# A two-layer MLP by Strassen products on one core: the second pair's first layer made two-level, its block sums made earlier by VectorE and GpSimd, rectifications moved to ScalarE

## The chip, the core and the metric

The kernel runs on one core of a Trainium2 chip. A core has TensorE (PE; the profile lists its weight loads apart, as PEld), VectorE (DVE), ScalarE (ACT), GpSimd (POOL) and SyncE (SP), whose queue issues most of the DMAs here. Each engine works through its own instructions in order and waits on semaphores for the others. The metric is device time in microseconds; lower is better. Three runs of the kernel before took 793.56, 793.8 and 795.42 us, median 793.8.

## What is computed

The reference is a block of linear attention followed by a Fourier mixing layer with an MLP. Cut to what matters here:

```python
x = lightning_attn(q, k, v, lam)            # (4, 8, 768, 64) -> (4, 768, 512)
u = x + real(fft(fft(x, axis=1), axis=2))
un = (u - mean(u)) / sqrt(var(u) + 1e-06)   # over the last axis
out = u + np.maximum(un @ w_ch1, 0.0) @ w_ch2   # w_ch1 512 x 2048, w_ch2 2048 x 512
```

All of it is float32. The change concerns the last line alone, for the last two thirds of the rows.

## The kernel before

**Stages.** Attention, Fourier mixing and normalisation give 12 groups of 256 rows each (`ORDER`). Four of them (`PLAIN`) go through the MLP by ordinary matmuls while the mixing of the others still runs (`mlp`). The other eight (`LATE`) are kept in DRAM, normalised (`utd`) and not (`ud`), and are worked at the end as four pairs, j = 0 to 3, of 512 rows. From here on the chip does nothing but the MLP of these pairs.

**One level.** A pair is one matrix product per layer, and each matrix is cut in 2 x 2 blocks. `PRODUCTS` names the seven block products of Strassen's scheme (in Winograd's form), each of a block or block sum of one matrix with one of the other. `combine_weights` makes the weights' block sums once: `s2.A` holds the first layer's blocks (w1: a11, a12, a22, s1 to s4), `s2.B` the second's.

**Two levels.** A product can itself be done by seven smaller ones. That needs sums of quarters of every one of the seven operands (S1, S2, S4 of the left, T1, T2, T4 of the right; the fourth, S3 or T3, replaces a quarter). `DEEP = 2` tells which pairs do the first layer in one level: j < DEEP does (`first_layer`), j >= DEEP uses two levels (`deep_first`). The second layer always has two levels (`deep_second`). `seven` is the frame of a two-level product: seven steps m = 0 to 6 in three PSUM banks X, Y, Z. X takes m = 0, 2, 4, 6 one on top of the other, and after each step the bank is read out by ScalarE (a copy, where the destination is fresh) or VectorE (an addition).

**first_layer(j).** Its loop runs over HF = 8 slices i of the hidden units. A slice has seven products of two matmuls each (128x128 by 128x256; the profile records two passes of each, so 28 records a slice). In PE's order a slice runs: a11, a12 (of slice i), s4, a22*t4 (of slice i-1, in `finish`), s2, s3, s1 (of slice i). Bank X collects a11, s2, s1, s4, and ScalarE copies X out after each of the first three; Z collects s3 and a22*t4; Y takes a12. VectorE adds Y to a11 (L915), Z to a22 (L924) and later Z to a12 (L903), rectifies each in place (L916, L925, L904: `tensor_scalar` with max), and makes s1 = a21 + a22 and s3 = a11 - a21 (L905, L906) from a21, which ScalarE rectified out of X into an SBUF tile `sv` (L901). In slices 5 to 7 VectorE also does `split` (L856, 128x512: a quarter difference in place), and at the end `prepare_a(j, 0)` and `prepare_a(j, 1)` (L870, L872, L874), the quarter sums that the first two second-layer products need.

**The weights' quarter sums.** They serve every pair and are made once, by GpSimd, beside the first layers: `keep_sums` (L727, L731) for the second layer's seven operands in pair 0's first layer, `keep_sums_w` (L747) for the first layer's seven in pair 1's. Each is four 128x512 operations for a product, seven products, so 28. Three results of four (all four in `keep_sums_w`) go through six rotating buffers `tx` to DRAM (`td`, `sd`) by SP's queue, and come back by `load_three` just before use. S3 goes back into a quarter of the weights (`place_sums_w`). GpSimd starts after `begun`, a copy of one column that waits for pair 0's first a11.

**Order.** `in_step` interleaves consecutive products: while product q does its steps 4 to 6, product q+1 does its first. So PE's order at the start of a second layer is, with qP,m for product P and step m: q0,0; q0,1; q0,2; q0,3; q1,0; q0,4; q1,1; q0,5; q1,2; q0,6; q1,3; q2,0; q1,4; and so on, eight records each. `late` puts pair 0's first and second layer, pair 1's first and second layer, and the deep pairs 2 and 3 behind each other. Tile pools with one buffer (`y2`, the pair's output tile that `open_y` takes; `ur`, its input) make the next user of a buffer wait until the last one is through.

Of the kernel before, what the change touches and what calls it, by code (L numbers as in the profile page):

```python
# [76 lines left out]
def kernel(  # L77
# [642 lines left out]
    s2.td = []  # L720
    s2.begun = wt.tile([128, 1], F32, name="begun")

    def keep_sums(k):

        pin = tc.keep_in_program_order
        B11, B12, B21, B22 = quarters_b(s2.B[PRODUCTS[k][1]])
        pin(nc.gpsimd.tensor_tensor(B12, B22, B12, op=SUB))  # L727
        T1, T2, T4 = t = [new(s2.yp, [128, HF // 2, HM // 2], "tx", bufs=6) for _ in range(3)]
        s2.td.append([dram.tile([128, HF // 2, HM // 2], F32, name=f"td{k}{i}") for i in range(3)])
        for i, o, x, y, op in ((1, T2, B12, B11, ADD), (0, T1, B22, T2, SUB), (2, T4, B21, T2, SUB)):  # L730
            pin(nc.gpsimd.tensor_tensor(o, x, y, op=op))  # L731
            nc.sync.dma_start(s2.td[k][i], o)

    s2.sd = []

    def quarters_w(t):

        return [t[:, k, f:f + FH // 2] for f in (0, FH // 2) for k in range(2)]

    def keep_sums_w(k):  # L740

        pin = tc.keep_in_program_order
        A11, A12, A21, A22 = quarters_w(s2.A[PRODUCTS[k][0]])
        S3, S2, S1, S4 = [new(s2.yp, [128, FH // 2], "tx", bufs=6) for _ in range(4)]
        s2.sd.append([dram.tile([128, FH // 2], F32, name=f"sd{k}{i}") for i in range(4)])
        for i, o, x, y, op in ((3, S3, A11, A21, SUB), (1, S2, A22, S3, SUB), (0, S1, S2, A11, ADD), (2, S4, A12, S2, SUB)):
            pin(nc.gpsimd.tensor_tensor(o, x, y, op=op))  # L747
            nc.sync.dma_start(s2.sd[k][i], o)

    def place_sums_w():  # L750

        for k, (a, _) in enumerate(PRODUCTS):
            nc.sync.dma_start(quarters_w(s2.A[a])[2], s2.sd[k][3])
# [22 lines left out]
    DEEP = 2  # L776
# [107 lines left out]
    def first_layer(j):  # L884
# [11 lines left out]

        def finish(i, X, Z):
            a11, a12, a22, s1, s3 = (h[n][:, :, i, :] for n in ("a11", "a12", "a22", "s1", "s3"))
            prod(X, "s4", "b22", i, False)
            a21 = new(s2.hp, [128, G, 128], "sv", bufs=3)  # L900
            nc.scalar.activation(a21, two(X), AF.Relu)  # L901
            prod(Z, "a22", "t4", i, False)
            V.tensor_tensor(a12, two(Z), a12, op=ADD)  # L903
            V.tensor_scalar(a12, a12, 0.0, None, op0=ALU.max)  # L904
# [3 lines left out]
        last = None  # L908
        for i in range(HF):
            a11, a12, a22 = (h[n][:, :, i, :] for n in ("a11", "a12", "a22"))  # L910
            X, Y, Z = (bank()[:, 0:G * 128] for _ in range(3))
# [4 lines left out]
            V.tensor_scalar(a11, a11, 0.0, None, op0=ALU.max)  # L916
            if last:
                finish(*last)
            prod(X, "s2", "t2", i, False)
            nc.scalar.copy(a12, two(X))  # L920
            prod(Z, "s3", "t3", i, True)
            prod(X, "s1", "t1", i, False)
            nc.scalar.copy(a22, two(X))
            V.tensor_tensor(a22, two(Z), a22, op=ADD)  # L924
            V.tensor_scalar(a22, a22, 0.0, None, op0=ALU.max)  # L925
            last = (i, X, Z)
            if j < min(DEEP, 2) and i < len(PRODUCTS):
                if i == 0:
                    tc.keep_in_program_order(nc.gpsimd.tensor_copy(s2.begun, h["a11"][:, 0, 0, 0:1]))
                (keep_sums, keep_sums_w)[j](i)  # L930
# [7 lines left out]
        run(prepare_a(j, 0))  # L938
        finish(*last)
        run(prepare_a(j, 1))  # L940
# [22 lines left out]
    def deep_first(j, k):  # L963
# [37 lines left out]

        if k == 1:
# [145 lines left out]
    def late():  # L1148
        for j in range(PAIRS):
            if j < DEEP:  # L1150
                open_pair(j)
                if j == 0:
                    run(inputs(0))
                first_layer(j)
                if j + 1 < DEEP:
                    in_step(second_layer(j) + [(inputs(j + 1), iter(()))])
# [116 lines left out]
```

## Time and profile before

The profiled execution took 796.12 us; its span, from the first to the last instruction, is 793.9 us, and the granted TensorE clock was 0.995 on average.

| engine | busy us | share of the span | instructions |
|---|---|---|---|
| PE | 763.4 | 96% | 5616 |
| DVE | 585.5 | 74% | 1148 |
| ACT | 225.4 | 28% | 532 |
| POOL | 197.6 | 25% | 198 |

| stretch, us of the span | length | PE busy | DVE busy | ACT busy | POOL busy |
|---|---|---|---|---|---|
| pair 0 first layer, 425.34 to 476.31 | 50.97 | 50.67 | 48.26 | 12.27 | 39.03 |
| pair 0 second layer, 476.31 to 518.29 | 41.98 | 41.98 | 30.98 | 3.99 | 6.56 |
| pair 1 first layer, 518.29 to 568.49 | 50.20 | 50.20 | 43.66 | 12.28 | 38.76 |
| pair 1 second layer, 568.49 to 607.79 | 39.30 | 39.30 | 31.30 | 3.99 | 7.08 |

The granted clock is 1.00 in all four stretches. A row of the timeline gives start, duration, engine, line, operation, output and input, shape and count, and in brackets the idle time of the engine before it with what ended that. [...]

### The profile page before, as it was taken

To read this page: it belongs to the slowest core of one execution; us is meant where nothing else is said; L and a number is where in the kernel's file an instruction comes from. 1 tells how busy PE (TensorE), PEld (TensorE's weight loads), DVE (VectorE), ACT (ScalarE), POOL (GpSimd) and SP (SyncE) were. 2 spreads that over 40 slices of the span, in tenths; PEclk is the share of its full clock that TensorE was granted. 3 is DMA by queue.
4 is the path that set the end of the run, shared out by engine and by line. 5 is a ranking of instruction groups with operands and counts; after the bars stand their busy time and mean duration, and the time that the engine had idled before them with its cause. 6 is when DMAs were issued, how large, how long until landed. Compare 5 with 4: busy or idle time off the path is not lost.

```text
span 793.9 us, 14617 instructions
## 1 busy us (share of the span) xinstructions
PE 763.4 (96%) x5616; PEld 646.3 (81%) x5616; DVE 585.5 (74%) x1148; ACT 225.4 (28%) x532; POOL 197.6 (25%) x198
## 2 busy tenths in 40 slices
PE   6889989999999999998999999999999999999995
PEld 5768766758585867767946889988999999999995
DVE  6899889675844582345698998769966699758983
ACT  3665443335621221321201221022211342034300
POOL 3223330011111110211004950279205001220021
PEclk9999999999999999999999999999999999999998
DMA  9978723238842147441233374345944455455341
GB/s 243 247 165 245 196 85 129 85 74 205 227 116 77 54 79 146 108 143 64 54 66 107 133 246 162 97 167 191 348 147 153 150 174 185 129 176 186 121 131 70
DMA packets 152331, 116.80 MB, mean 147 GB/s; under 512 B 113998, under 2 KB 113998, under 8 KB 152262
## 3 DMA queue, kind: packets, MB, share of 16 engines
q1 hardware_dynamic: 147120, 103.39, 45.8%
q0 software_dynamic: 2112, 6.69, 2.4%
q10 hardware_dynamic: 3030, 5.78, 2.0%
q8 instruction: 45, 0.74, 0.4%
q14 instruction: 24, 0.20, 0.1%
HBM read 83.58 MB, written 32.25 MB: 146 GB/s over the span
## 4 chain that ended last, share of the span: by engine, by line
PE 78%; DVE 9%; DMA 4%; issue 4%; ACT 1%; POOL 1%; SPq 0%; POOLq 0%; ACTq 0%; DVEq 0%
PE p L1046 21%; PE p L891 12%; PE p L976 11%; PE pm L658 10%; PE pm L644 9%; PE pa L525 3%; PE pa L300 3%; PE pa L341 3%; DMA x<-xb,ix 2%; PE pa L335 2%; PE pa L276 1%; PE pa L357 1%; PE pa L320 1%; DVE sc L304 1%; PE pa L281 1%
## 5 line engine op out<-in xcount | busy, mean ns | idle before, releaser
L644 PE MATMUL pm<-ut,w 128*128 128x256 f32 x512 | 119.7, 384 | 0.0
L658 PE MATMUL pm<-w,hr 128*128 128x512 f32 x256 | 115.7, 596 | 0.2 <-DVE w L227 0.2
L644 PEld LDWEIGHTS pm<-ut,w 128*128 128x128 f32 x512 | 95.6, 192 | 14.2 <-issue 2.1
L658 PEld LDWEIGHTS pm<-w,hr 128*128 128x128 f32 x256 | 46.6, 190 | 49.3 <-issue 48.0
L1060 POOL TENSOR_TENSOR y<-y,u 128x512 f32<-128x512 f32 x12 | 18.8, 1569 | 199.2 <-DVE y L1069 156.8
L1046 PE MATMUL p<-tx,sx 128*128 128x128 f32 x416 | 54.9, 275 | 0.0
L1046 PEld LDWEIGHTS p<-tx,sx 128*128 128x128 f32 x416 | 50.6, 192 | 0.0
L891 PE MATMUL p<-ur,w 128*128 128x256 f32 x192 | 46.9, 379 | 0.1
L272 POOL TENSOR_TENSOR kd<-k,decay 128x512 f32<-128x512 f32 x20 | 22.0, 1100 | 95.3 <-PE pa L320 48.7
L1052 ACT COPY y<-p 128x128 f32<-128x128 f32 x48 | 12.8, 266 | 104.1 <-PE p L1046 103.8
L1054 DVE TENSOR_TENSOR y<-p,y 128x128 f32<-128x128 f32 x92 | 25.5, 286 | 22.5 <-PE p L1046 15.9
L891 PEld LDWEIGHTS p<-ur,w 128*128 128x128 f32 x192 | 36.3, 190 | 5.7 <-issue 0.5
L304 DVE TENSOR_TENSOR sc<-pa,decay 128x512 f32<-128x512 f32 x48 | 31.5, 683 | 8.1 <-PE pa L300 7.9
L1046 PE MATMUL p<-w,ha 128*128 128x128 f32 x288 | 37.4, 275 | 0.0
L300 PEld LDWEIGHTS pa<-qT,kT 64*128 64x128 f32 x384 | 26.1, 193 | 13.4 <-ACT qT L283 7.4
L652 ACT ACTIVATE hr<-pm 128x256 f32<-128x256 f32 x44 | 16.7, 385 | 66.2 <-PE pm L644 66.0
L1046 PEld LDWEIGHTS p<-w,ha 128*128 128x128 f32 x288 | 35.0, 192 | 0.2
L300 PE MATMUL pa<-qT,kT 64*128 64x128 f32 x384 | 30.8, 292 | 3.3 <-ACT qT L283 3.1
L341 PE MATMUL pa<-sc,v 128*64 128x128 f32 x384 | 30.0, 279 | 4.0 <-DVE sc L304 3.8
L558 POOL TENSOR_SCALAR ve<-mv 128x2 f32<-128x2 f32 x12 | 3.4, 286 | 122.3 <-DVE mv L555 122.3
L891 PE MATMUL p<-sx,w1s 128*128 128x256 f32 x128 | 32.9, 380 | 0.2 <-DVE sx L794 0.2
L650 DVE TENSOR_SCALAR hr<-pm 128x256 f32<-128x256 f32 x20 | 8.3, 414 | 32.8 <-PE pm L644 32.8
(234 smaller groups left out, 1736.6 us busy)
## 6 DMA issues: line engine op xcount, KB each, us to landing
tx<-td SPq DMA_DIRECT2D x84, 256.0 KB, 2.7
raw<-in_moe_w_ch_dram SPq DMA_DIRECT2D x32, 512.0 KB, 4.0
tx<-sd SPq DMA_DIRECT2D x42, 256.0 KB, 2.7
sd<-tx SPq DMA_DIRECT2D x28, 256.0 KB, 2.1
k<-in_k_dram SPq DMA_DIRECT2D x24, 256.0 KB, 5.2
q<-in_q_dram SPq DMA_DIRECT2D x24, 256.0 KB, 4.3
v<-in_v_dram SPq DMA_DIRECT2D x24, 256.0 KB, 5.0
td<-tx SPq DMA_DIRECT2D x21, 256.0 KB, 2.0
```

The source lines that it names most:

```text
L272: nc.gpsimd.tensor_tensor(kd, kt, kpow, op=ALU.mult)
L300: mm(pss[hi][:, hp, :], lhsT=kT[HD[hi], hp, :], rhs=qT[HD[hi], hp, :], start=True, stop=True)
L304: nc.vector.tensor_tensor(t, pss[hi], decay[:, hi::2, :], op=ALU.mult)
L341: mm(po[HD[hi], hp, :], lhsT=vt[:, 2 * hp + hi, :], rhs=sc[hi][:, hp, :], start=(c == 0 and hp == 0), stop=(hp == HP - 1), skip_group_chec ...
L525: mm = nc.tensor.matmul(ps[:, n, :], lhsT=piece(a, i, n), rhs=cs[0:rows, a, i in (2, 3), n, :], start=(a == 0), stop=(a == 1))
L644: nc.tensor.matmul(ps, lhsT=w1[:, c, 128 * fc:128 * fc + 128], rhs=ut[:, c, :], start=(c == 0), stop=(c == KO - 1))
L658: nc.tensor.matmul(ps, lhsT=hr[(fc - f0) // 4][:, fc % 4, 128 * i:128 * i + 128], rhs=w2[:, fc, :], start=(fc == f0), stop=(fc == f1 - 1))
L891: nc.tensor.matmul(ps, lhsT=s2.A[a][:, kt, 128 * i:128 * i + 128], rhs=U[b][:, kt, :], start=(first and kt == 0), stop=(kt == 1), skip_gro ...
L976: nc.tensor.matmul(ps[:, 128 * i:128 * i + 128], lhsT=ab[m][0][:, 128 * i:128 * i + 128], rhs=ab[m][1], start=(start and i == 0), stop=Tru ...
L1046: nc.tensor.matmul(ps[:, 0:HM // 2], lhsT=ab[m][0][i], rhs=ab[m][1][:, i, :], start=(start and i == 0), stop=(i == HF // 2 - 1), skip_grou ...
L1054: V.tensor_tensor(o, ps[:, 0:HM // 2], o, op=ADD)
L1060: nc.gpsimd.tensor_tensor(o, y, u, op=ADD)
```

## The change

- `DEEP` becomes 1: pair 1 is a deep pair like 2 and 3, and `first_layer` runs for pair 0 alone.
- The first layer's quarter sums (`sd`) have to exist one pair earlier. `block_sums` replaces `keep_sums` and `keep_sums_w`. In pair 0's first layer GpSimd still makes the second layer's 28, and then those of the first layer's products 3 and 4 (8 more). VectorE makes those of products 0, 1 and 5 (12 operations, two in each of slices 1 to 6). Those of products 2 and 6 are made by GpSimd when pair 1's first two deep products start (8 operations).
- The first-layer sums don't use `tx`. They are staged in a `y2` tile (`spare_y`), four slots that every product reuses, and go to DRAM from there on SP's queue.
- In `first_layer` the three rectifications of a slice move from VectorE to ScalarE (`relu`, 128x256 in SBUF). a21 is no longer put in SBUF: ScalarE rectifies it into the second half of bank X, and VectorE's s1 and s3 read it there.

```diff
--- before.py
+++ after.py
@@ -717,40 +717,42 @@
 
         return [t[:, i:i + HF // 2, m:m + HM // 2] for i in (0, HF // 2) for m in (0, HM // 2)]
 
-    s2.td = []
+    s2.td, s2.sd = {}, {}
     s2.begun = wt.tile([128, 1], F32, name="begun")
 
-    def keep_sums(k):
-
-        pin = tc.keep_in_program_order
-        B11, B12, B21, B22 = quarters_b(s2.B[PRODUCTS[k][1]])
-        pin(nc.gpsimd.tensor_tensor(B12, B22, B12, op=SUB))
-        T1, T2, T4 = t = [new(s2.yp, [128, HF // 2, HM // 2], "tx", bufs=6) for _ in range(3)]
-        s2.td.append([dram.tile([128, HF // 2, HM // 2], F32, name=f"td{k}{i}") for i in range(3)])
-        for i, o, x, y, op in ((1, T2, B12, B11, ADD), (0, T1, B22, T2, SUB), (2, T4, B21, T2, SUB)):
-            pin(nc.gpsimd.tensor_tensor(o, x, y, op=op))
-            nc.sync.dma_start(s2.td[k][i], o)
-
-    s2.sd = []
-
     def quarters_w(t):
 
         return [t[:, k, f:f + FH // 2] for f in (0, FH // 2) for k in range(2)]
 
-    def keep_sums_w(k):
-
-        pin = tc.keep_in_program_order
-        A11, A12, A21, A22 = quarters_w(s2.A[PRODUCTS[k][0]])
-        S3, S2, S1, S4 = [new(s2.yp, [128, FH // 2], "tx", bufs=6) for _ in range(4)]
-        s2.sd.append([dram.tile([128, FH // 2], F32, name=f"sd{k}{i}") for i in range(4)])
-        for i, o, x, y, op in ((3, S3, A11, A21, SUB), (1, S2, A22, S3, SUB), (0, S1, S2, A11, ADD), (2, S4, A12, S2, SUB)):
-            pin(nc.gpsimd.tensor_tensor(o, x, y, op=op))
-            nc.sync.dma_start(s2.sd[k][i], o)
+    SHAPES = ([128, FH // 2], [128, HF // 2, HM // 2])
+
+    def block_sums(eng, layer, k, stage=None, inside=False):
+
+        q = Q11, Q12, Q21, Q22 = (quarters_w, quarters_b)[layer]((s2.A, s2.B)[layer][PRODUCTS[k][layer]])
+        d = (s2.sd, s2.td)[layer][k] = [dram.tile(SHAPES[layer], F32, name=f"{'st'[layer]}d{k}{i}") for i in range(4)]
+        if layer == 0:
+            todo = ((3, Q11, Q21, SUB), (1, Q22, 3, SUB), (0, 1, Q11, ADD), (2, Q12, 1, SUB))
+        else:
+            todo = ((3, Q22, Q12, SUB), (1, 3, Q11, ADD), (0, Q22, 1, SUB), (2, Q21, 1, SUB))
+        t = {3: q[2 - layer]} if inside else {}
+        for i, x, y, op in todo:
+            if i not in t:
+                t[i] = stage[i] if stage else new(s2.yp, SHAPES[layer], "tx", bufs=6)
+            x, y = (t[z] if isinstance(z, int) else z for z in (x, y))
+            tc.keep_in_program_order(eng.tensor_tensor(t[i], x, y, op=op))
+            if i < 3 or not inside:
+                nc.sync.dma_start(d[i], t[i])
+            yield 1.0
+
+    def spare_y():
+
+        t = new(s2.yp, [128, 2, G, DM], "y2").rearrange("p a b c -> p (a b c)")
+        return [t[:, 512 * i:512 * i + 512] for i in range(4)]
 
     def place_sums_w():
 
-        for k, (a, _) in enumerate(PRODUCTS):
-            nc.sync.dma_start(quarters_w(s2.A[a])[2], s2.sd[k][3])
+        for k in (0, 1, 3, 4, 5):
+            nc.sync.dma_start(quarters_w(s2.A[PRODUCTS[k][0]])[2], s2.sd[k][3])
 
     def load_u(j, queue=nc.sync):
 
@@ -773,7 +775,7 @@
         pass
 
     PAIRS = len(LATE) // 2
-    DEEP = 2
+    DEEP = 1
     pairs = [Pair() for _ in range(PAIRS)]
     for P_ in pairs:
         P_.pre_a, P_.pre_b, P_.pre_w = {}, {}, {}
@@ -894,40 +896,52 @@
         def two(t):
             return t.rearrange("p (s k) -> p s k", s=G)
 
+        def relu(t):
+            nc.scalar.activation(t, t, AF.Relu)
+
         def finish(i, X, Z):
             a11, a12, a22, s1, s3 = (h[n][:, :, i, :] for n in ("a11", "a12", "a22", "s1", "s3"))
-            prod(X, "s4", "b22", i, False)
-            a21 = new(s2.hp, [128, G, 128], "sv", bufs=3)
-            nc.scalar.activation(a21, two(X), AF.Relu)
+            prod(X[:, 0:G * 128], "s4", "b22", i, False)
+            a21 = two(X[:, G * 128:2 * G * 128])
+            nc.scalar.activation(a21, two(X[:, 0:G * 128]), AF.Relu)
             prod(Z, "a22", "t4", i, False)
             V.tensor_tensor(a12, two(Z), a12, op=ADD)
-            V.tensor_scalar(a12, a12, 0.0, None, op0=ALU.max)
             V.tensor_tensor(s1, a21, a22, op=ADD)
             V.tensor_tensor(s3, a11, a21, op=SUB)
 
         last = None
+        place = spare_y()
+        sums = chain(block_sums(V, 0, k, place) for k in (0, 1, 5))
         for i in range(HF):
             a11, a12, a22 = (h[n][:, :, i, :] for n in ("a11", "a12", "a22"))
-            X, Y, Z = (bank()[:, 0:G * 128] for _ in range(3))
+            whole = bank()
+            X, Y, Z = whole[:, 0:G * 128], *(bank()[:, 0:G * 128] for _ in range(2))
             prod(X, "a11", "b11", i, True)
             nc.scalar.copy(a11, two(X))
             prod(Y, "a12", "b21", i, True)
             V.tensor_tensor(a11, two(Y), a11, op=ADD)
-            V.tensor_scalar(a11, a11, 0.0, None, op0=ALU.max)
             if last:
+                relu(h["a22"][:, :, i - 1, :])
                 finish(*last)
+                next(sums, None)
             prod(X, "s2", "t2", i, False)
             nc.scalar.copy(a12, two(X))
+            relu(a11)
             prod(Z, "s3", "t3", i, True)
             prod(X, "s1", "t1", i, False)
             nc.scalar.copy(a22, two(X))
+            if last:
+                relu(h["a12"][:, :, i - 1, :])
             V.tensor_tensor(a22, two(Z), a22, op=ADD)
-            V.tensor_scalar(a22, a22, 0.0, None, op0=ALU.max)
-            last = (i, X, Z)
-            if j < min(DEEP, 2) and i < len(PRODUCTS):
-                if i == 0:
-                    tc.keep_in_program_order(nc.gpsimd.tensor_copy(s2.begun, h["a11"][:, 0, 0, 0:1]))
-                (keep_sums, keep_sums_w)[j](i)
+            if last:
+                next(sums, None)
+            last = (i, whole, Z)
+            if i == 0:
+                tc.keep_in_program_order(nc.gpsimd.tensor_copy(s2.begun, h["a11"][:, 0, 0, 0:1]))
+            if i < len(PRODUCTS):
+                run(block_sums(nc.gpsimd, 1, i, inside=True))
+            else:
+                run(block_sums(nc.gpsimd, 0, 3, place))
             if i == HF - 3:
                 load_x(j)
             if i == HF - 2:
@@ -936,7 +950,10 @@
             if i > HF // 2:
                 split(h[("a11", "a12", "s3")[i - HF // 2 - 1]])
         run(prepare_a(j, 0))
+        relu(h["a22"][:, :, HF - 1, :])
         finish(*last)
+        relu(h["a12"][:, :, HF - 1, :])
+        run(block_sums(nc.gpsimd, 0, 4, place))
         run(prepare_a(j, 1))
         if j + 1 < PAIRS:
             load_u(j + 1)
@@ -999,6 +1016,10 @@
                 if relu:
                     nc.scalar.activation(o_, o_, AF.Relu)
 
+        if j == DEEP and k < 2:
+            if k == 0:
+                s2.place = spare_y()
+            run(block_sums(nc.gpsimd, 0, (2, 6)[k], s2.place, inside=True))
         if k == 1:
             yield from quarter_sum(T, T, a11)
         elif k == 2:
@@ -1146,14 +1167,9 @@
                         del live[q]
 
     def late():
-        for j in range(PAIRS):
-            if j < DEEP:
-                open_pair(j)
-                if j == 0:
-                    run(inputs(0))
-                first_layer(j)
-                if j + 1 < DEEP:
-                    in_step(second_layer(j) + [(inputs(j + 1), iter(()))])
+        open_pair(0)
+        run(inputs(0))
+        first_layer(0)
         in_step(second_layer(DEEP - 1) + [w for j in range(DEEP, PAIRS) for w in deep_pair(j)])
```

## The prediction, made before the result was known

> **What bounds the kernel now.** I read the page first (PE 96% busy), then PE's waits from 425 us to the end, then PE's timeline for the length of each stage.
>
> ```profile
> PE p L891 <- DVE sx L794: 0.2, 1, 0.2
> ```
>
> That is the whole list of waits that PE had in 365 us: the stage is bound by PE, all else is cover. So the change can win only by giving PE less to do, and it loses whatever it makes PE wait. The timeline shows what there is to win. It has step q0,2 of each pair's second layer (the first with `tx` as weights), and q1,2 of pair 0:
>
> ```profile
> 476.31 1.06 PE L1046 MATMUL p<-tx,sx 128*128 128x128 f32 x8
> ...
> 481.67 1.06 PE L1046 MATMUL p<-tx,sx 128*128 128x128 f32 x8
> ...
> 568.49 1.06 PE L1046 MATMUL p<-tx,sx 128*128 128x128 f32 x8
> ...
> 655.14 1.06 PE L1046 MATMUL p<-tx,y 128*128 128x128 f32 x8
> ...
> 742.69 1.06 PE L1046 MATMUL p<-tx,y 128*128 128x128 f32 x8
> ```
>
> From pair 0 to pair 1, which is one level and then two, is 568.49 - 476.31 = 92.18 us; from deep pair 2 to deep pair 3 is 742.69 - 655.14 = 87.55. **Removed: 92.18 - 87.55 = 4.63 us.** The records agree: 224 at 0.2157 us (0.863 for four) are 48.3, 392 at 0.1117 (0.8935 for eight) are 43.8. Nothing larger can be won.
>
> **What pair 0's first layer must now carry.** It is the stage with the fullest VectorE (48.26 of 50.97 us), and VectorE and GpSimd hold each other up there. VectorE's timeline, a normal slice and two `split`s:
>
> ```profile
> 451.39 0.41 DVE L915 TENSOR_TENSOR ha<-p,ha 128x256 f32<-128x256 f32 x1
> 451.83 0.91 DVE L916 TENSOR_SCALAR ha<-ha 128x256 f32<-128x256 f32 x1
> 452.67 0.41 DVE L905 TENSOR_TENSOR hs<-sv,ha 128x256 f32<-128x256 f32 x1
> 453.00 1.48 DVE L906 TENSOR_TENSOR hs<-ha,sv 128x256 f32<-128x256 f32 x1
> 454.41 0.41 DVE L903 TENSOR_TENSOR ha<-p,ha 128x256 f32<-128x256 f32 x1
> ...
> 462.53 1.75 DVE L856 TENSOR_TENSOR ha<-ha 128x512 f32<-128x512 f32 x1
> ...
> 469.16 0.68 DVE L856 TENSOR_TENSOR ha<-ha 128x512 f32<-128x512 f32 x1
> ```
>
> Operations that read PSUM (L915, L903, also L924) always take 0.41. Those wholly in SBUF take 0.29, 0.42 or 0.68 alone (the rows after 468.4, when GpSimd is done) but 0.91, 1.48 or 1.75 beside GpSimd. They end just after a GpSimd operation ends: they wait for its end, up to 1.06 (1.48 - 0.42). GpSimd pays too:
>
> ```profile
> 462.42 1.31 POOL L727 TENSOR_TENSOR w<-w 128x512 f32<-128x512 f32 x1
> 463.81 1.60 POOL L731 TENSOR_TENSOR tx<-w 128x512 f32<-128x512 f32 x1
> ...
> 521.29 1.26 POOL L747 TENSOR_TENSOR tx<-w 128x512 f32<-128x512 f32 x1
> ...
> 526.48 1.45 POOL L747 TENSOR_TENSOR tx<-w 128x512 f32<-128x512 f32 x1
> ...
> 598.68 1.71 POOL L1060 TENSOR_TENSOR y<-y,u 128x512 f32<-128x512 f32 x1
> ```
>
> Undisturbed, four take 526.48 - 521.29 = 5.19, so 1.30 each. The one that had to let the 0.68 `split` through took 1.60 for 1.26, 0.34 more; another with a 512-wide VectorE sum beside it 1.71, 0.45 more.
>
> *VectorE, per slice.* Out go three rectifications (0.91 each) and, since a21 now lies in PSUM, the waits of L905 and L906. What stays are five PSUM operations, 5 x 0.41 = 2.1 us, and two 512-wide sums, 0.68 to 1.75 each: 3.4 to 5.6 of a slice's 6.04. That fits.
>
> *ScalarE, per slice.* Four operations of 0.37 become seven, 2.6 of 6.04. But they come between VectorE and PE. In the changed order ScalarE does: rectify a11, rectify a21, rectify the last slice's a12, copy a12 out of X; PE's s1 needs that copy. From the slice's start: s4 ends at 2.59 (three products of 0.863), ScalarE sees it 0.21 later (its copy at 437.54 follows a product that ended at 437.33), a21 is done at 3.18, s1, s3 and a12 on VectorE (0.34 apart, the last 0.42 long) at 4.31, a12's rectification at 4.73, the copy at 5.07, and PE wants it at 5.18. **Slack 0.1 us.** It also holds only if VectorE starts a11 by 1.95. Before it stands the second sum: a22 ends at 1.03, so the sum ends at 1.6 alone or 2.6 after a full wait, up to 0.65 late. Four GpSimd operations and two sums let through (4 x 1.30 + 2 x 0.40) are 6.0, just a slice, so the two should settle beside each other: I take 0 for slices 2 to 5, and keep 4 x 0.65 = 2.6.
>
> *Slices 6 and 7.* Here a `split` stands behind the sum and must wait for another whole GpSimd operation: 1.07 + 0.60. a11 starts at 3.2 to 4.3 in place of 1.95: 1.2 to 2.3 late each, and PE with it. I take 1.4 each, **2.8**. Behind them a22 of slice 7, which PE's last first-layer product waits for, stands in VectorE's queue after product 0's three sums, two of which wait for GpSimd: about 1.0 more. Before, GpSimd was done at 468.4, and these rows ran at 0.68. So VectorE alone makes PE **3.8** late.
>
> *GpSimd.* 28 operations become 36. It starts at 430.0 (429.71 before, plus one rectification on ScalarE). 36 x 1.30 = 46.8; in that time 19 512-wide VectorE operations must be let through (12 sums, 3 splits, 4 sums of `prepare_a`), at 0.34 to 0.45, say 0.40: 7.6. **End at 484.4** (482.9 to 485.4).
>
> *Who waits for that.* The slots lie in the `y2` tile, and pair 0's output takes it next. In the built order the first write to it, ScalarE's copy after q1,0, waits for GpSimd and for the DMAs of product 4's sums:
>
> ```profile
> 479.24 0.27 ACT L1052 COPY y<-p 128x128 f32<-128x128 f32 x1 [0.68 <-PE p L1046]
> ```
>
> and such a DMA takes 2.1 us from issue to landing (the page's list of DMA issues):
>
> ```profile
> sd<-tx SPq DMA_DIRECT2D x28, 256.0 KB, 2.1
> ```
>
> Then 479.24 becomes 484.4 + 2.1 = 486.5. PE's q1,2 needs bank X back: 486.5 + 0.27 + 0.2 for semaphores = 487.0 against 481.67, **5.3 late**. Behind that copy stand all of ScalarE's further copies for products 0 and 1. The 3.8 lies within the 5.3, since GpSimd works on while PE waits: the larger counts.
>
> *Edits at nothing.* The 20 first-layer writes beside the 21 old ones on SP: covered by 256 KB in 2.1 us against 1.3 to 1.7 a GpSimd operation on 16 engines, and a slot is written again only four operations later. SP's reads for product 2 now stand behind the last write, so they are issued near 485; q2,2 needs them at 487.92 + 5.3 = 493.2, even behind the 1 MB of `ur` (5.7 to land). If that cover went, about 1. Pair 1's first products: the eight GpSimd operations for products 2 and 6 wait until pair 0's stores have left `y2` (at the same point of pair 2 they were issued at 616.30, so near 619, 11 us into the deep pair), end near 630, and product 2's reads are needed at 630 to 635: covered by 3 us; bounds 0 to 2. The 28 GpSimd operations of pair 1's first layer go; PE never waited for them.
>
> **Sum.** -4.63 + 5.3 = +0.7. Against the profiled execution: 796.12 to 796.8; the runs' median is 2.3 lower, so 793.8 + 0.7 = **794.5 us**.
>
> [...]
>
> **Rivals.**
> *A, the gain is kept.* If VectorE's sums slip into GpSimd's gaps as L904 does (its neighbours on GpSimd take 1.31 to 1.33, 0.05 more), GpSimd ends at 430.0 + 46.8 + 19 x 0.05 = 477.8, its last write lands before 480, and the copy is in time. Left are the splits at half price, 1.4: 793.8 - 4.6 + 1.4 = 790.6. For it: two of VectorE's four waits in a slice go. Against it: 462.53 and 463.81.
> *B, ScalarE's chain decides: slower.* The slack of 0.1 is gone in every slice, if the sum's wait is the long one of L906: 4 x 0.65, two split slices at 2.3, 1.0 at the join: 8.2, above the 5.3 of GpSimd, which by then is done. 793.8 - 4.6 + 8.2 = 797.4. It decides as soon as the sum waits over 0.35 us in most slices.
> *C, the change's second half doesn't hold:* product 2's sums come too late in pair 1, with VectorE's quarter sums held up beside them. 2 on top of the forecast: 796.5.
>
> **Chances.** Forecast 0.56 (by itself 792.5 to 796.2), A 0.18, B 0.18, C 0.08. A measurement of this kernel tells 0.3% (2.4 us) from no change. Forecast within it, A beyond it below, B and C above: faster 0.18, same 0.56, slower 0.26. The range takes in A's time and B's, 790.6 to 798.0; outside lie the better half of A, the worse half of B and the tails, 2 in 10.
>
> **What would show it.** PE's waits in pair 0's first layer name ScalarE's a12 copy in slices 6 and 7 only (forecast) or in all (B). GpSimd's last first-layer sum ends near 484; the copy to `y` is near 486.5 and named as what PE waits for, or not late at all (A). From q0,2 of pair 0 to that of pair 1 PE needs 87 plus the join's stalls. Wrong altogether would be a stall after pair 0's second layer, or another stage than these changed.

## The result and the profile after

The changed kernel took **807.7 us** (median of six runs, 805.4 to 809.86) against 795.09 (793.56 to 796.06) for the kernel before on the same chip: a ratio of 1.0157, 95% interval 1.0138 to 1.0177. The forecast of 794.5, with its range of 790.6 to 798.0, was wrong: most of its chance stood on no difference. The profiled execution took 807.34 us, with a span of 805.6 and a mean granted clock of 0.989 (0.995 before).

Read it in the same order as before. PE's waits from 420 us to the end; where there was one row of 0.2 us, the changed kernel has four:

```profile
PE p L893 <- ACT ha L928: 7.3, 3, 5.3
PE p L1067 <- ACT y L1073: 4.9, 1, 4.9
PE p L893 <- DVE ha L935: 0.3, 1, 0.3
PE p L893 <- DVE sx L796: 0.2, 1, 0.2
```

The columns are the total, how often, and the longest. The first row is PE's s1 product waiting for ScalarE's copy of a12 (L928) in slices 5 to 7; the second is q1,2 waiting for ScalarE's copy into `y`. Both kinds of wait were in the forecast, with 2.8 us (slices 6 and 7) and 5.3 us; the longest one, in slice 5, was not. The two large ones in PE's timeline:

```profile
465.93 2.07 PE L893 MATMUL p<-sx,w1s 128*128 128x256 f32 x4 [5.26 <-ACT ha L928]
...
497.94 2.03 PE L1067 MATMUL p<-tx,sx 128*128 128x128 f32 x8 [4.93 <-ACT y L1073]
```

PE's timeline has q0,2 of pairs 0, 1 and 2 at:

```profile
487.49 1.06 PE L1067 MATMUL p<-tx,sx 128*128 128x128 f32 x8
...
580.97 1.06 PE L1067 MATMUL p<-tx,y 128*128 128x128 f32 x8
...
668.52 1.06 PE L1067 MATMUL p<-tx,y 128*128 128x128 f32 x8
```

From pair 1 to pair 2 it takes 87.55 us (668.52 - 580.97), as a deep pair did before: the saving is there, and nothing is lost after pair 0. Pair 0 itself reaches q0,2 at 487.49 instead of 476.31, 11.2 late, and loses 5 more at q1,2. So the first layer of pair 0 is the place. VectorE's timeline there, from the middle of slice 4 on (the bracket gives the idle time ahead of a row and what ended it):

```profile
452.56 0.42 DVE L908 TENSOR_TENSOR ha<-p,ha 128x256 f32<-128x256 f32 x1
455.75 1.67 DVE L742 TENSOR_TENSOR y<-y,w 128x512 f32<-128x512 f32 x1 [2.77 <-DMA sd<-y]
457.34 0.41 DVE L935 TENSOR_TENSOR ha<-p,ha 128x256 f32<-128x256 f32 x1
461.27 1.72 DVE L742 TENSOR_TENSOR y<-w,y 128x512 f32<-128x512 f32 x1 [3.52 <-DMA sd<-y]
462.91 0.41 DVE L922 TENSOR_TENSOR ha<-p,ha 128x256 f32<-128x256 f32 x1
```

GpSimd holds VectorE up here too (the sums, L742, take 1.67 and 1.72 us; the 512-wide `split` took 0.68 alone), but the larger part, 2.77 and 3.52 us, is idle time before the sums: they wait for their **slot**, that is for the DMA that carries the slot's last content to DRAM. The a22 and a11 additions (L935, L922) stand behind them, ScalarE's rectification and copy behind those, and PE behind the copy. Why is that DMA late? SP's queue in the same stretch:

```profile
455.55 3.34 SPq L744 DMA_DIRECT2D td<-tx  x3
458.98 0.38 SPq L744 DMA_DIRECT2D sd<-y  x1
461.13 3.33 SPq L744 DMA_DIRECT2D td<-tx  x3
464.55 0.38 SPq L744 DMA_DIRECT2D sd<-y  x1
```

SP issues in order: the write of VectorE's fifth sum, which was made by 447.56, was issued at 464.55, behind nine `td<-tx` and two `sd<-y` writes. The `td<-tx` writes wait for GpSimd's sums (32.8 us in 18 waits from 424 to 500 us), three of them for a whole product, and behind three of them the scheduler put **one** `sd<-y` write: one in 5.6 to 5.9 us. VectorE makes two sums in a slice of 6.04. With four slots the surplus is used up in slice 4, and from there VectorE runs at the pace of SP, which runs at the pace of GpSimd. GpSimd's own first-layer sums use the same slots and meet the same queue, and ScalarE's first copy into the `y2` tile comes last:

```profile
479.70 1.27 POOL L742 TENSOR_TENSOR y<-w1s 128x512 f32<-128x512 f32 x1 [10.01 <-DMA sd<-y]
...
493.68 1.71 POOL L742 TENSOR_TENSOR y<-w1s,y 128x512 f32<-128x512 f32 x1
```

```profile
497.62 0.27 ACT L1073 COPY y<-p 128x128 f32<-128x128 f32 x1 [7.88 <-DMA sd<-y]
```

That is the row whose forerunner was at 479.24. GpSimd had been done with the second layer's 28 operations at 469.69, but waited 10.01 us for a slot and ended at 495.39, not 484.4. And there was one loss that no term of the forecast named. Busy time of PE, PEld, DVE, ACT and POOL by stretch, then the granted clock, DMA share and GB/s:

```profile
460.50:465.90 5.40, 0.16 (x1) 0.00 (x0) 3.13 (x5) 1.36 (x4) 5.24 (x5) 0.81 0.49 180
465.90:470.97 5.07, 5.04 (x12) 4.06 (x13) 1.83 (x2) 1.16 (x3) 3.71 (x3) 0.52 1.01 322
...
497.90:501.30 3.40, 3.36 (x16) 3.36 (x17) 3.38 (x6) 0.27 (x1) 0.00 (x0) 0.52 0.99 375
```

After each of its two idle times of about 5 us PE ran at half clock: 12 records took 5.04 instead of 2.59 us, 16 took 3.52 (the row cuts the last short) instead of 1.79, together 4.18 us.

The account, from PE's first row that waits for `DVE sx` (427.76 before, 427.91 after) to its row of ten records in pair 3's second layer (739.11 and 752.49): 311.35 became 324.58, **+13.23**. Idle 12.55 (12.78 less the 0.23 at the start), half clock 4.18, less work -4.53: 12.2. The last 1.0 is in the restarts, where a first group of four takes 1.13 instead of 1.03 and comes later than the idle time shown. From the end of PE's last product to the end of the span it takes 6.46 us instead of 8.17, 1.71 less, and the stretch starts 0.15 later. Together that is +11.67, the difference of the two spans (805.57 and 793.90). The runs' medians differ by 12.6.

I use this stretch for every kernel below, because it leaves out what comes before: the start of the stage lies between 424.90 and 429.60 us in the fourteen profiles, and all of that is ahead of the code that the change touches. It also leaves out the tail, which is 6.2 to 6.5 us in every kernel with a two-level pair 1, and 8.17 before and 7.80 in e4. The medians contain both.

### The profile page after: what moved, and what is told of

It reads as the page before. It is cut to its first block, busy times and chain, and to the rows that moved or that the text cites. A ratio compares the mean times of both kernels' runs of the same rounds, so it can differ in the third digit from the quotient of the medians.

```text
span 805.6 us, 14997 instructions
## 1 busy us (share of the span) xinstructions
PE 764.7 (95%) x5784; PEld 651.1 (81%) x5784; DVE 577.6 (72%) x1127; ACT 239.7 (30%) x556; POOL 191.8 (24%) x195
## 4 chain that ended last, share of the span: by engine, by line
PE 72%; DVE 9%; DMA 6%; POOL 6%; issue 4%; ACT 2%; SPq 0%; POOLq 0%; ACTq 0%; DVEq 0%
PE p L1067 20%; PE p L993 16%; PE pm L658 10%; PE pm L644 8%; PE pa L341 3%; PE pa L525 3%; PE pa L300 3%; POOL tx L742 3%; DMA x<-xb,ix 2%; DMA sd<-y 2%; PE pa L335 2%; PE pa L276 1%; PE pa L320 1%; DVE sc L304 1%; PE pa L357 1%
## 5 line engine op out<-in xcount | busy, mean ns | idle before, releaser
L1002 DVE TENSOR_TENSOR ha<-p,ha 128x512 f32<-128x512 f32 x60 | 39.9, 684 | 9.0 <-PE p L993 8.8
L1002 DVE TENSOR_TENSOR hs<-p,hs 128x512 f32<-128x512 f32 x39 | 26.2, 683 | 13.5 <-PE p L993 13.5
L993 PE MATMUL p<-sx,tx 128*128 128x128 f32 x264 | 33.9, 275 | 0.0
L341 PEld LDWEIGHTS pa<-sc,v 128*64 128x64 f32 x384 | 23.8, 142 | 10.3 <-DVE sc L304 7.4
```

What stands on the lines that cost most here:

```text
L341: mm(po[HD[hi], hp, :], lhsT=vt[:, 2 * hp + hi, :], rhs=sc[hi][:, hp, :], start=(c == 0 and hp == 0), stop=(hp == HP - 1), skip_group_chec ...
L993: nc.tensor.matmul(ps[:, 128 * i:128 * i + 128], lhsT=ab[m][0][:, 128 * i:128 * i + 128], rhs=ab[m][1], start=(start and i == 0), stop=Tru ...
L1002: V.tensor_tensor(o, p, o, op=ADD)
```

## The experiments

The theory at the outset: **SP's order** makes slots late, and through them VectorE, ScalarE and PE. Rival 1: VectorE and GpSimd hold each other up, and the slots are only where it shows. Rival 2: the slots' place in the `y2` tile is what hurts. Rival 3: the DMA engines have too many bytes to move (their busy share was 0.90 in 467 to 487 us).

| kernel | median us | before, same chip | ratio, 95% interval | stretch, us (before: 311.35) |
|---|---|---|---|---|
| changed kernel | 807.7 | 795.09 | 1.0157 (1.0138 to 1.0177) | 324.58 |
| e1: SP's order mended | 795.59 | 794.5 | 1.0018 (0.9993 to 1.0042) | 316.31 |
| e2: own slots | 803.59 | 794.5 | 1.0134 (1.0113 to 1.0155) | 320.29 |
| e3: both | 795.79 | 794.5 | 1.0025 (1.0008 to 1.0041) | 311.54 |
| e4: rectifications alone | 794.8 | 794.9 | 0.9994 (0.9977 to 1.0012) | 311.89 |
| e5: eight slots | 802.17 | 794.5 | 1.0116 (1.0090 to 1.0142) | 321.40 |
| e6: e3, splits moved | 794.51 | 794.9 | 0.9991 (0.9970 to 1.0012) | 311.74 |
| e7: e3, GpSimd relieved | 797.12 | 794.9 | 1.0031 (1.0009 to 1.0054) | 314.81 |
| e8: e6 and e7 | 794.69 | 794.9 | 0.9987 (0.9975 to 0.9999) | 313.02 |
| e9: e8, sums earlier | 796.02 | 794.76 | 1.0025 (1.0008 to 1.0042) | 313.54 |
| e10: sums spread | 792.82 | 796.08 | 0.9952 (0.9936 to 0.9968) | 310.59 |
| e11: e10, built order | 800.67 | 794.2 | 1.0068 (1.0043 to 1.0092) | 319.89 |
| e12: e10 again | 792.58 | 794.2 | 0.9969 (0.9955 to 0.9983) | 310.58 |

**e1, SP's order mended.** One line of the changed kernel: the writes of the sums keep the order in which the program names them.

```diff
-                nc.sync.dma_start(d[i], t[i])
+                tc.keep_in_program_order(nc.sync.dma_start(d[i], t[i]))
```

> Only the order of SP's queue differs from the changed kernel: behind each three td<-tx writes come two sd<-y writes, where the scheduler had put one. Theory (the queue's order): VectorE and GpSimd find their slots free, the DVE and POOL waits on sd<-y in 424 to 500 us (11.3 and 12.4 us now) fall under 2 us, GpSimd's last first-layer sum ends near 485 instead of 495.4, PE's idle time in slices 4 to 7 (8 us now) falls to 0 to 3 us, the granted clock stays near 1.00 there, and ScalarE's wait for y (7.9 us) shrinks to the 3 to 5 us I forecast: 793 to 797 us. Rival 1 (VectorE and GpSimd slow each other, and the slots are only where it shows): the stalls stay, above 803. Rival 2 (only the slots' place in y2 hurts): the stall before q1,2 stays, 803 or more. Rival 3 (the DMA engines have too many bytes to move): the same bytes, so the same waits, above 804.

795.59 us, at 1.0018 not to be told from before. SP's queue now:

```profile
448.42 3.35 SPq L744 DMA_DIRECT2D sd<-y  x2
451.86 2.26 SPq L744 DMA_DIRECT2D td<-tx  x3
454.42 3.34 SPq L744 DMA_DIRECT2D sd<-y  x2
```

VectorE's waits on `sd<-y` are gone from the list altogether (11.3 us before the edit). The two longest of PE's waits from 420 us on:

```profile
PE p L1067 <- ACT y L1073: 3.3, 1, 3.3
PE p L893 <- ACT ha L928: 2.4, 2, 1.5
```

11.5 of the 12.6 us are explained by the order of one queue: (807.7 - 795.09) - (795.59 - 794.5) = 11.5. Rival 1 and rival 3 would have left the stalls; they fall as the main cause, since the work of both engines and all the bytes are the same. One wait outlived the edit: GpSimd waited 4.5 us for a slot ahead of product 4's sums (until 483.17), so it ended at 490.42 and not near 485; the first of the writes that free these slots was issued at 476.71, behind six `tx<-td` loads on SP. The stretch of this profile is 5 us above before, though the median is only 1.1 above it. This profiled execution was one of four in ten of e1 with a mean clock of 0.991 to 0.994 (797.7 to 801.8 us); the six with 0.999 took 793.7 to 795.9. Behind the stall before q1,2, 3.3 us here, the clock is 0.50 from 493.97 to 497.39, which costs PE at most 1.7 us; the two groups suggest that it falls in some executions and not in others. They lie further apart than that, and what else parts them is not shown: only this execution has a trace.

**e2, own slots.** Order as built; the slots lie in pair 0's `u2` tiles, which are loaded later.

```diff
-        place = spare_y()
+        u2 = [new(s2.yp, [128, G, DM], "u2", bufs=2) for _ in range(2)]
+        place = [t[:, i] for t in u2 for i in range(G)]
...
-            if i == HF - 3:
-                load_x(j)
...
         elif k == 1:
+            if j < DEEP:
+                load_x(j)
```

> The sums' four slots lie in pair 0's u tiles, loaded later, and no longer in the y tile; SP's order of td and sd writes is as built. Theory (the queue's order): the stalls of slices 4 to 7 (8 us idle and 2.5 us of halved clock) stay, because VectorE still waits for slots, and only the idle time before q1,2 (5.1 us and 1.7 us of halved clock) goes: 807.7 - 6.8 = 801, 799 to 803. Rival 2 (slots in y2 alone): nearly all of the loss goes, 789 to 793. Rival 1 (contention): like the theory here, 799 to 803. Rival 3 (bytes): 801 to 806, with the u loads in the way later.

803.59, 0.6 us above what the order theory gave. PE's waits for `ACT ha` stay (7.1 us, three times, the longest 5.3) with the half clock behind them; the wait for the `y` copy is gone, and a new one of 2.4 us for VectorE in the second layer has come. Rival 2 falls: the slots' place is worth about 3.5 of the 12.6 us (12.6 less 803.59 - 794.5).

**e3, both edits.**

> Both edits: two sd writes behind each three td writes, and slots outside the y tile. Theory (the queue's order): neither VectorE nor ScalarE waits, what is left is the 4.5 us that PE has less to do and up to 3 us of waiting in the split slices: 789 to 794, against 795 for the kernel before. Rival 1 (contention): 798 to 802. Rival 3 (bytes): above 799.

795.79, 2 us above the expectation's upper end, though its stretch is only 0.19 above before. PE's timeline, all that is left of idle time beyond 0.3 us:

```profile
467.99 1.13 PE L893 MATMUL p<-sx,w1s 128*128 128x256 f32 x4 [0.90 <-ACT ha L929]
...
475.76 1.13 PE L893 MATMUL p<-sx,w1s 128*128 128x256 f32 x4 [1.46 <-ACT ha L929]
...
488.26 1.16 PE L1066 MATMUL p<-w,sx 128*128 128x128 f32 x8 [1.55 <-DVE t L1074]
```

Set row by row against PE's timeline before, this kernel is on time to 0.01 us through slice 5 and the first half of slice 6, then 1.16 late, from slice 7 on 2.88, and from q0,6 on 4.70; the 4.53 of less work bring it back to 0.2. So with the order mended and the slots moved, the change only breaks even in the stretch (its runs are 0.08 to 0.41% longer than those before): its saving goes to PE's waits for VectorE. I had expected up to 3 us of waiting, and it was 4.7.

**e4, one part alone.** The kernel before, with the rectifications on ScalarE and a21 in PSUM, as in the change; nothing else.

> The kernel before with one part of the change alone: the rectifications of the first layer on ScalarE and a21 in PSUM; pair 1 stays one level, no sum moves. Theory: this part costs nothing and wins nothing, because PE did not wait in that stage before (0.2 us in all) and ScalarE's longer chain still ends before PE wants its copy: 793 to 796, ratio 0.998 to 1.002. Rival (the chain through ScalarE is too long by itself): PE waits for ACT ha in slices 1 to 7, 797 or more.

794.8 against 794.9: no difference, and PE's longest new wait is 0.2 us. ScalarE's slack of 0.1 us, which I had worked out, is enough.

**e5, eight slots.** SP's order as built; VectorE's products 0 and 5 in the `y2` tile, product 1 and GpSimd's two in the `u2` tiles.

```diff
-        sums = chain(block_sums(V, 0, k, place) for k in (0, 1, 5))
+        first = spare_y()
+        sums = chain(block_sums(V, 0, k, place if k == 1 else first) for k in (0, 1, 5))
```

> SP's order as built (one sd write behind three td writes), but eight slots instead of four, none of which pair 0's y products wait for late: VectorE's products 0 and 5 in the y tile, its product 1 and GpSimd's two in the u tiles. Theory (the queue's order, felt through the slots): by slice 6 VectorE has made 12 sums and SP has written 5 or 6, so 6 or 7 are outstanding, fewer than eight: VectorE's waits on sd<-y fall under 2 us and the stalls of slices 4 to 7 go, though SP is as late as before; the y copy waits for the last sum in the y tile, written about 485, so 0 to 2 us there: 790 to 795. Rival 1 (contention): stalls stay, 799 to 803. Rival 3 (bytes): above 799.

802.17: the expected time is missed by 7 us, and why is instructive. VectorE has no wait for a slot any more, and the stalls of slices 6 and 7 are those of e3 (0.90 and 1.47). That is the link from the slots to VectorE. But the writes are as late as ever, and now the `y` tile waits for all of them:

```profile
491.02 2.08 PE L1067 MATMUL p<-tx,sx 128*128 128x128 f32 x8 [8.99 <-ACT y L1073]
```

The last of its slots' writes is issued at 487.06. I had put it near 485 and took 0 to 2 us for the copy. More buffers moved the wait to the next reader of the buffers; they did not shorten it.

**e6, splits moved.** e3 with each `split` of slices 5 to 7 in the place of a sum behind s3, where VectorE has 2.4 us, and no longer between a22 and a11; the twelfth sum comes behind the loop.

```diff
                 finish(*last)
-                next(sums, None)
+                if i > HF // 2:
+                    split(h[("a11", "a12", "s3")[i - HF // 2 - 1]])
+                else:
+                    next(sums, None)
...
-            if i > HF // 2:
-                split(h[("a11", "a12", "s3")[i - HF // 2 - 1]])
```

> The kernel with the mended SP order and own slots (795.8, of which 2.9 us of PE's time were lost in slices 6 and 7 and 1.8 later), and the three splits moved: in slices 5 to 7 a split takes the place of the sum behind s3, where VectorE has 2.4 us until its next job, and no longer stands between a22 and a11, where it has 1.05. One sum a slice is left there, the twelfth comes after the loop. Theory (the 2.8 us that I forecast for the splits): the 2.9 us fall under 1.0, the wait for VectorE in the second layer (1.8) stays or grows a little: 793 to 794.5. Rival (what is late is VectorE as a whole beside GpSimd, wherever the split stands): the stalls stay at 2 to 3 us, 795 to 797.

794.51, 0.9991. The two stalls of the split slices shrink from 0.90 and 1.46 to one of 0.48, so what stands ahead of a11 in VectorE's queue there was the cause. The edit changes two things, the splits' place and the sums, of which slices 5 and 6 have one less each; which of them counts is not shown. What was won came back in the second layer: GpSimd, now waiting for VectorE's last sum, worked until 493.5, and PE waited 1.16 and 2.38 us there for VectorE, whose 512-wide sums again took up to 1.75.

**e7, GpSimd relieved.** e3, but VectorE makes the sums of products 0, 3 and 4, and GpSimd those of 2, 1, 5 and 6 in pair 1, each ahead of its use.

```diff
-        sums = chain(block_sums(V, 0, k, place) for k in (0, 1, 5))
+        sums = chain(block_sums(V, 0, k, place) for k in (0, 3, 4))
...
-            else:
-                run(block_sums(nc.gpsimd, 0, 3, place))
...
-        if j == DEEP and k < 2:
+        if j == DEEP and k < 4:
...
-            run(block_sums(nc.gpsimd, 0, (2, 6)[k], s2.place, inside=True))
+            run(block_sums(nc.gpsimd, 0, (2, 1, 5, 6)[k], s2.place, inside=True))
```

> The kernel with the mended SP order and own slots, and GpSimd's eight sums of the first layer (products 3 and 4) taken out of the stage: VectorE makes those of products 0, 3 and 4, GpSimd those of 2, 1, 5 and 6, each one product or more ahead of its use, in pair 1. GpSimd is then done near 472 instead of 486.9. Theory (VectorE is late from slice 7 on because GpSimd holds it up): slice 6's 1.2 us stay, slice 7's 1.7 shrink to 0 to 1, the 1.8 us of the second layer go: 4.7 lost become 1.2 to 2.2, 792 to 794. Rival (the queue's order once more, in pair 1: sd writes stand behind td loads on SP, so a product's sums come late): PE waits for tx in pair 1's products 1 or 5, 796 to 805.

797.12, within the rival's range but not by its mechanism. In pair 0 the waits of the second layer went, as expected, but slice 7's stall shrank only to 1.29. In pair 1 PE waited 2.29 and 2.08 us, not for a load but for VectorE.

**e8, e6 and e7 together.**

> Both of the last two edits on top of the mended SP order and own slots. Theory: PE waits in the first layer and in the second for less than 1 us in all, and the 4.5 us that PE has less to do are nearly all won: 790.5 to 792.5, ratio 0.995 to 0.998. Rival (sums late in pair 1): 794 to 803. If clock drops after idle times and not the sums made the spread of the runs, the runs here lie closer together than those of the kernel with the built order.

794.69, 0.9987: pair 0 loses only 0.47 us, and pair 1 2.45 and 2.09. VectorE's quarter sums in pair 1 (L1013), while GpSimd makes the moved sums:

```profile
543.66 1.75 DVE L1013 TENSOR_TENSOR hs<-hs,hs 128x512 f32<-128x512 f32 x1
...
547.02 1.75 DVE L1013 TENSOR_TENSOR hs<-hs,hs 128x512 f32<-128x512 f32 x1
```

Three in a row (the one left out as well) take 1.75 each. The time is the rival's, the mechanism is not: no load was late. Its ten runs lie within 3.66 us, the changed kernel's six within 4.46; that doesn't settle what the clock adds to the spread. Rival 1, dismissed as the main cause, is what limits the mended kernel.

**e9, the moved sums earlier.** e8, with products 2 and 1 in pair 0's second layer behind GpSimd's additions to `y` (slots in `u2`), 5 and 6 behind pair 1's inputs.

```diff
+        if j < DEEP and k in (3, 4):
+            if k == 3:
+                u2 = [new(s2.yp, [128, G, DM], "u2", bufs=2) for _ in range(2)]
+                s2.place = [t[:, i] for t in u2 for i in range(G)]
+            run(block_sums(nc.gpsimd, 0, (2, 1)[k - 3], s2.place, inside=True))
```

> The kernel with the mended SP order, own slots, moved splits and four products' sums outside the first layer, but these sums earlier: GpSimd makes those of products 2 and 1 in pair 0's second layer as soon as its last addition to y is done (about 511 us), in slots in pair 0's u tiles, which are free by then, and those of 5 and 6 behind pair 1's inputs. In the run before, GpSimd made them from 524 to 554 us, and PE waited 2.45 and 2.09 us for VectorE at 549 and 555, whose 512-wide sums (L1013 there) took 1.75 beside GpSimd and 0.68 without it. Theory (VectorE's sums wait for whole GpSimd operations, and PE for VectorE): GpSimd is done near 540, these sums take 0.68, the two stalls fall from 4.5 to under 1 us in all, and the time to 790.5 to 793 (ratio 0.995 to 0.9985). Rival (these stalls are VectorE's own load in pair 1's first layer, whoever works beside it): the stalls stay at 3 us or more, 794 to 796. Rival (the sums in the second layer only move the loss there): PE waits for VectorE between 500 and 525 us, 793 to 797.

796.02, 1.0025: the second rival's time. The quarter sums behind GpSimd's end (543.8) are at their length alone again, and the two stalls of e8 are gone:

```profile
546.08 0.68 DVE L1013 TENSOR_TENSOR hs<-hs,hs 128x512 f32<-128x512 f32 x1
```

But eight GpSimd operations in the second layer make PE wait 2.07 us for VectorE at 518, and 1.25 for a `tx<-sd` load at 524, which stood on SP behind the writes of product 1's sums.

**e10, the sums spread.** One group of four GpSimd operations at a time: VectorE products 0, 4 and 5 (slots in `y2`); GpSimd product 3 in the first layer, 2 in the second layer, 1 and 6 in pair 1. Splits moved, order mended.

```diff
-        sums = chain(block_sums(V, 0, k, place) for k in (0, 3, 4))
+        first = spare_y()
+        sums = chain(block_sums(V, 0, k, first) for k in (0, 4, 5))
...
+            else:
+                run(block_sums(nc.gpsimd, 0, 3, place))
...
-            run(block_sums(nc.gpsimd, 0, (5, 6)[k], s2.place, inside=True))
+            run(block_sums(nc.gpsimd, 0, (1, 6)[k], s2.place, inside=True))
...
-        if j < DEEP and k in (3, 4):
+        if j < DEEP and k == 3:
...
+            run(block_sums(nc.gpsimd, 0, 2, s2.place, inside=True))
```

> The sums spread thinner. First layer: VectorE makes those of products 0, 4 and 5 (slots in the y tile), GpSimd those of 3 (slots in the u tiles). Pair 0's second layer: GpSimd those of 2, right behind its additions to y. Pair 1: GpSimd those of 1 and 6 behind pair 1's inputs. Moved splits and the mended SP order as before. In the last run four sums more (product 1's) in the second layer made PE wait 2.07 us for VectorE at 518 and 1.25 for a tx load that stood behind their writes on SP at 524. Theory (each group of four GpSimd operations beside VectorE's busy stretches holds VectorE up, and the writes hold up SP): with one group there the waits at 518 and 524 fall under 1 us in all, the first layer keeps its 0.5, the y copy waits less than 1: 790.5 to 793, ratio 0.995 to 0.9985. Rival (one group in the first layer behind slice 7 is enough to hold VectorE up there, as in the runs where GpSimd worked until 487): 1.5 us or more lost at 480 to 490, 793 to 795.

**792.82 against 796.08: 0.9952 (0.9936 to 0.9968), faster than both kernels.** PE waits 0.50, 1.26 and 0.61 us. The rival came in part: the longest wait is for slice 7's a22 on VectorE,

```profile
477.52 1.13 PE L893 MATMUL p<-sx,w 128*128 128x256 f32 x4 [1.26 <-DVE ha L940]
```

and VectorE works beside GpSimd's one group there: it is busy for 4.52 us of 470 to 475 and for all 5.00 of 475 to 480, GpSimd for 4.84 and 3.25. Of the gain, only 0.8 us are in the stretch; the tail behind PE's last product is 1.6 us shorter (6.53 against 8.17), and why is open.

**e11, the same with the built order, and e12, the same again.** e11 undoes e1's line in e10 and nothing else.

> The last kernel (spread sums, 0.995 of the kernel before) with one line undone: the sums' writes are no longer held in program order on SP, so that the scheduler again puts one sd write behind three td writes. Work, slots and the other engines' orders stay. Theory (the queue's order is what made the change slow): VectorE waits for its slots from slice 4 on, PE is idle for 7 to 9 us in slices 4 to 7 and runs at half clock for some of it, and the copy to y waits as well: 799 to 807. Rival (with the sums spread, the order no longer matters): within 1.5 us of the last kernel.

> The kernel with the spread sums once more, beside the one with the built order: its gain over the kernel before should come again, 0.993 to 0.998 of it. If it was that chip's, the ratio is 0.998 or more.

e12 took 792.58 (0.9969, 0.9955 to 0.9983): the gain comes again, on another chip. e11 took 800.67: one line, **8.1 us**. PE's two longest waits in e11:

```profile
PE p L893 <- ACT ha L933: 5.3, 1, 5.3
PE p L994 <- DMA tx<-sd: 3.0, 1, 3.0
```

The first is slice 5's stall of the changed kernel (5.26 there), with half clock behind it; the second is a load in pair 1 that stands behind sums' writes on SP. Slices 4 to 7 lose 5.6 us of idle time and not the 7 to 9 expected, and the copy to `y` did not wait: the time was as expected, in part by another path. So the order costs on both sides: writes behind other writes hold up the slots, loads behind writes hold up PE directly.

## Why the prediction was wrong

**The step that failed** is "Edits at nothing": *"The 20 first-layer writes beside the 21 old ones on SP: covered by 256 KB in 2.1 us against 1.3 to 1.7 a GpSimd operation on 16 engines, and a slot is written again only four operations later."* It priced the writes by how long a transfer takes. What counted was where they stood: a DMA is issued when the one before it on SP has been, and that one waited for GpSimd. It takes 2.4 us (the median of the changed kernel's 26), but was issued up to 17 us after its sum was there (VectorE's fifth: made by 447.56, issued at 464.55). I had counted the new writes, and had not written down the order in which SP would issue them, nor set its rate (one in 5.6 to 5.9 us) against VectorE's (two in 6.04). e1 and e11 put this step at 11.5 and 8.1 us.

The other steps:

- *Removed, 4.63.* Right: 4.53 by the records, and 87.55 us from pair 1 to pair 2.
- *Slices 2 to 5 at nothing, ScalarE's slack 0.1.* Right: e3 is on time to 0.01 us there, and e4 shows the rectifications to cost nothing. Rival B is refuted.
- *Split slices, 2.8.* Right in sum (1.16 + 1.72 = 2.88 in e3); e6, which moves them and has one sum less in slices 5 and 6, brings it down to 0.48. The 1.0 at the join behind them was not there in e3; 1.26 at that place showed in e10, whose queue there is another.
- *The 3.8 within the 5.3, "since GpSimd works on while PE waits".* Not so in the changed kernel: GpSimd stood still for 10.01 us, and PE's idle time in slices 4 to 7 (0.31, 5.26, 1.60 and 0.45 us) came on top of the 4.93 at q1,2.
- *GpSimd's end, 484.4.* With the order mended and own slots (e3) it ended at 486.86 in a stage that began 1.11 later, so 485.7, with a wait of 1.2 in it. The sum of operations was right; what failed in the changed kernel was the assumption that GpSimd would never wait.
- *The copy into `y`, 5.3 late.* The mechanism was right, the size followed from GpSimd's end: in the changed kernel the copy came at 497.62 instead of 486.5.
- *The half clock.* No term for it: 4.18 us.
- *Rival A, 790.6:* not reached; the best version found is 3.3 (e10) and 1.6 us (e12) below before. *Rival C:* refuted for the change as built, no wait in pair 1; with four products' sums there (e7, e8) its mechanism, VectorE's quarter sums held up by GpSimd, cost 4.4 to 4.5 us.

With the failed step put right, the forecast's time would have stood: 794.5 was forecast, +0.7, and e1 measures +1.1. That is partly luck: in e1's profile PE is idle for 6.2 us in the stretch and not 5.3, up to 1.7 more go to the half clock, and the tail, which the forecast left as it was, is 1.7 us shorter.

What stays open: why e3's median lies 1.3 above before though its stretch and its shorter tail (6.44 us) come out 1.5 below (one profile against eight runs), and why the tail is 1.6 to 2.0 us shorter in the kernels with a two-level pair 1 (in the changed kernel the `out_dram` transfer in the chain that ended last takes 2.76 us, before it took 4.62; in e4 it takes 4.52).

## What to carry to other kernels

When a change adds DMAs to a queue that issues in order, write down the queue's built order around the new ones and ask for each entry what it waits for: here the new transfers left at the pace of the slowest wait ahead of them, one in 5.6 to 5.9 us, though one takes 2.4 us. A wait for a buffer whose content only has to be stored away is a sign of this; more buffers pass it on to the next reader (e5), one line of order removes it (e1, e11). And where two engines hold each other up, a total that fits is not enough: the work has to be spread into the stretches in which the other engine has room (e8, e9, e10).

## What the runs showed of the hardware

**After long idle times PE ran at half clock, and the price came on top of the stall.** In every case of the stage with 4.9 us of idle or more (5.26 and 4.93 in the changed kernel, 5.26 in e2, 8.99 in e5, 5.28 in e11) the granted clock fell to about 0.5 (0.52 in the changed kernel's two rows above, 0.56 in e2 from 461 to 467 us, 0.50 in e5 from 488 to 495 and in e11 from 465 to 470); in the changed kernel that cost 2.45 and 1.73 us more. In e1's profile 3.31 us were enough (0.50 from 495 to 497), and in the kernel before 2.04 us ahead of the row at 365.64 (0.51 from 366.3 to 369.6). Of the idle times between 2.0 and 2.5 us in the stretch, those of e2, e6, e7 and e8 (2.35, 2.38, 2.29 and 2.08, 2.45 and 2.09) left it at 1.00, and so did 3.05 us in e11 (before the row at 551.50), but 2.07 in e9 did not:

```profile
516.00:518.10 2.10, 0.07 (x1) 0.00 (x0) 2.10 (x5) 0.59 (x1) 2.02 (x2) 0.98 0.28 103
518.10:521.00 2.90, 2.86 (x13) 2.86 (x14) 2.90 (x3) 0.00 (x0) 2.90 (x3) 0.50 0.49 181
```

So in these runs the length alone doesn't decide, and what else does is not shown. In the changed kernel's trace, which records when the granted clock changes, the halvings begin at 26.99, 463.89, 498.03 and 801.82 us: the distances, 436.90, 34.14 and 303.79 us, are 128, 10 and 89 times 3.413. The first three last 3.41, 6.83 and 3.41 us; e5's in the stretch lasts 10.24.

**GpSimd and VectorE.** What the forecast went by held: a 512-wide sum of VectorE beside GpSimd costs GpSimd 0.33 to 0.45 (in the changed kernel 1.59 at 492.12 and 1.71 at 493.68, for 1.26 at 464.07), and costs VectorE 1.07 in the longest rows shown (1.75 at 543.66 in e8, for 0.68 at 546.08 in e9).
